# Batch 0's attention in the program's own order on four engines, with the w1 weight slices dealt out one per key chunk

## The chip, the core and the metric

The kernel runs on one core of one Trainium2 chip. The metric is the device time of one execution in microseconds (us), lower is better. Every kernel below was run beside runs of the kernel before on the same chip, and its result was compared with the reference. A run is counted as slow when it is more than 1.5% above the fastest run of the same kernel; such runs are left out of the ratios.

## The reference, cut to what matters

Two blocks follow each other. First comes attention over hashed buckets, 4 batches, 8 heads, 768 positions, head size 64; then a Fourier mixing block with a two-layer network on the 512 columns.

```
q_bits = (q @ proj > 0); k_bits = (k @ proj > 0)      # 6 bits each
mask   = bucket(q) == bucket(k)
scores = where(mask, scale * q @ k.T, -1e9)
attn   = softmax(scores)                               # over the keys
x      = attn @ v            -> (B, S, 512)
...
u  = x + real(fft2(x))                                 # over positions and columns
un = (u - mean(u)) / sqrt(var(u) + 1e-6)
out = u + relu(un @ w_ch1) @ w_ch2                     # w_ch1: 512 x 2048, float64 input
```

## The kernel before

Batch 0's attention goes through four head pairs, each in six key chunks. I call one chunk of one pair a "step"; there are 24. In each step the matrix engine (PE) forms scores for two query halves (`weigh`), ScalarE takes the exponential, and PE applies V to the chunk before it (`values`, in `finish`). For pairs 0 and 1 PE also adds up the softmax's row sums; for pairs 2 and 3 VectorE does, with two additions a step ("accumulations", tile `acc`). Beside this, `prepare` makes the next pair ready in pieces: transposes, bit products on PE, and their evacuation into `qkb` by VectorE.

The second weight of interest, w1, comes as float64, and is narrowed to float32 on the chip in 16 slices of 128 x 512 while batch 0's attention runs:

```
    def narrow(dst, raw, mask):
        lo, hi = (raw.rearrange("p (n w) -> p n w", w=2)[:, :, i] for i in range(2))
        ...
        nc.scalar.activation(mask, hi, AF.Abs)                        # ScalarE, 3 instructions
        nc.scalar.activation(mask, mask, AF.Abs, bias=mid[:, 0:1])
        nc.scalar.activation(mi, mask, AF.Sign, bias=mid[:, 1:2])
        nc.vector.tensor_scalar(di, hi, ...)                          # VectorE, 5 instructions
        nc.vector.scalar_tensor_tensor(mi, di, 1, mi, ...)
        nc.vector.scalar_tensor_tensor(di, hi, -(2**31), mi, ...)
        nc.vector.tensor_scalar(mi, di, -(1 << 23), None, ...)
        nc.vector.scalar_tensor_tensor(rest, lo.bitcast(U32), 2.0**-52, mask, ...)
        nc.gpsimd.tensor_tensor(dst, dst, rest, op=ALU.add)           # GpSimd, 1 instruction
```

After every fourth slice GpSimd adds the four slices up (`ws`), PE multiplies the sum with a constant matrix (`wm`, "the mean product"), and VectorE subtracts the result from the four slices. That removes the mean of each column of w1 once, instead of the mean of `u` in every row later.

```
        for i, (dst, src) in enumerate(slices):
            ...
                narrow(dst, raws[i % len(raws)].bitcast(I32), mask)
            fetch(i + depth, nc.gpsimd)
            yield
            if wsb is w1 and i % NDC == NDC - 1:
                f = i // NDC * WC
                ws = wt([P, WC], F32, "u", f"ws{f}", 2)
                for c in range(1, NDC):
                    nc.gpsimd.tensor_tensor(ws, ..., w1[:, c, f : f + WC], op=ALU.add)
                ps = pt([P, WC], f"wm{f}")
                nc.tensor.matmul(ps, mean, ws, start=True, stop=True)
                for c in range(NDC):
                    w = w1[:, c, f : f + WC]
                    nc.vector.tensor_tensor(w, w, ps, op=ALU.subtract)
                yield
```

The product's result `ps` comes from a PSUM pool of two buffers (`pt`), which it shares with the transposes, the bit products and the sums. The main loop runs the attention as a generator and takes one piece of w1 per step. The order in which each engine gets its instructions is then decided by a scheduler, not by this text:

```
    for b in range(B):
        for _ in attention(b):
            for _ in range(per_step):
                next(other, None)
```

Of the kernel before, what the change touches and what calls it, by code (L numbers as in the profile page):

```python
# [29 lines left out]
NDC = DM // P  # L30
# [435 lines left out]
def _main(  # L466
# [26 lines left out]
    def wt(shape, dtype, tag, name, bufs=2):  # L493
        return work.tile(shape, dtype, tag=tag, name=name, bufs=bufs)

    roomy = [True]
    turn = [0]

    def pt(shape, name):

        turn[0] += 1
        if roomy[0] and turn[0] % 2:
            if turn[0] % 4 == 1:
                return ps_o.tile(shape, F32, tag="o", name=name)
            return ps_sc.tile(shape, F32, tag="sc", name=name)
        return ps_1.tile(shape, F32, tag="ps", name=name)
# [14 lines left out]
    def load(n, others=nc.sync):  # L521
        b, t = divmod(n, NPAIR)
        for nm, src in (("q", q), ("k", k), ("v", v)):
            tag, bufs = ("vn", 2) if nm == "v" else ("qkn", 2)
            tl = wt([P, NT, 2, D], F32, tag, f"{nm}n{n}", bufs)
            for h in range(2):
                (nc.sync if nm == "q" else others).dma_start(
                    tl[:, :, h, :], src[b, 2 * t + h].rearrange("(p c) d -> p c d", c=NT)
                )
            nat[nm, n] = tl  # L530
# [49 lines left out]
    w1 = const.tile([P, NDC, DFF], F32, tag="w1", name="w1")  # L580
# [38 lines left out]
    def weights(wsb, wdr):  # L619

        wide = wdr.dtype == I64
        slices = [
            (wsb[:, c, f : f + WC], wdr[c * P : (c + 1) * P, f : f + WC])
            for f in range(0, wdr.shape[1], WC)
            for c in range(wdr.shape[0] // P)
        ]
        raws, masks = [], []
        if wide:
            zt = wt([P, 3, 2 * WC], F32, "z", f"zraw{wdr.shape[0]}", 1)
            raws += [zt[:, i] for i in range(3)]  # L630
            if wsb is w1:
                ft = wt([P, 12, WC], F32, "F", "fraw", 1)
                raws += [
                    ft[:, i : i + 2].rearrange("p i w -> p (i w)") for i in range(0, 8, 2)
                ]
                masks = [ft[:, i] for i in range(8, 12)]

        def fetch(i, queue):
            if i < len(slices):
                dst, src = slices[i]  # L640
                if wide:
                    raw = raws[i % len(raws)].bitcast(I32)
                    queue.dma_start(raw.bitcast(I64), src)
                else:
                    queue.dma_start(dst, src)

        depth = len(raws) or 4
        for i in range(depth):
            fetch(i, nc.sync if wsb is w1 else nc.gpsimd)
            if wsb is w1 and i == 1:  # L650
                load(1)
        yield
        for i, (dst, src) in enumerate(slices):
            if wide:
                mask = masks[i % 4] if masks else wt([P, WC], F32, "u", f"mask{i}", 2)
                narrow(dst, raws[i % len(raws)].bitcast(I32), mask)
            fetch(i + depth, nc.gpsimd)
            yield
            if wsb is w1 and i % NDC == NDC - 1:

                f = i // NDC * WC
                ws = wt([P, WC], F32, "u", f"ws{f}", 2)
                for c in range(1, NDC):
                    nc.gpsimd.tensor_tensor(
                        ws, ws if c > 1 else w1[:, 0, f : f + WC],
                        w1[:, c, f : f + WC], op=ALU.add,
                    )
                ps = pt([P, WC], f"wm{f}")
                nc.tensor.matmul(ps, mean, ws, start=True, stop=True)
                for c in range(NDC):  # L670
# [3 lines that stand above are left out]
# [128 lines left out]
    def values(n, c, pk, oos):  # L802

        for g in range(2):
            w = HALF + 1 - g
            for h in range(2):
                nc.tensor.matmul(  # L807
                    oos[g][h * D : (h + 1) * D, 0:w], nat["v", n][:, c, h, :],
                    pk[g][:, h, 0:w], start=(c == 0), stop=(c == NT - 1),
                )  # L810
# [44 lines left out]
    def attention(b):  # L855
        xs[b] = wt([P, NPAIR, S], F32, "x", f"x{b}")
        pending, scaling = [], [iter(())]

        def finish():
            n, c, pk, oos, accs, sums = pending.pop(0)  # L860
            for _ in scaling[0]:
                pass
            values(n, c, pk, oos)
            if sums is not None:
                for i in range(4):
                    nc.tensor.matmul(
                        sums[32 * i : 32 * i + 32, :], ones[:, 0:32],
                        pk[i // 2][:, i % 2, 0:HALF],
                        start=(c == 0), stop=(c == NT - 1),
                    )  # L870
            if c == NT - 1:
                scaling[0] = scale(n, oos, accs, sums)
                next(scaling[0], None)

        for t in range(NPAIR):
            n = NPAIR * b + t
            if 1 < n + 1 < NPAIR * B:
                load(n + 1)
            ahead = prepare(n + 1) if n + 1 < NPAIR * B else iter(())
            oos = [ps_o.tile([P, 512], F32, tag="o", name=f"oo{n}_{g}") for g in range(2)]  # L880
            accs = sums = None
            if n in SUMS:
                sums = pt([P, HALF], f"sums{n}")
            else:
                accs = [wt([P, 2, HALF], F32, "t3", f"acc{n}_{g}", 3) for g in range(2)]
            first = None
            for c in range(NT):
                new = [weigh(n, g, c) for g in range(2)]
                if c == 0:
                    first = new  # L890
                elif accs:
                    for g in range(2):
                        nc.vector.tensor_tensor(  # L893
                            accs[g], first[g][:, :, 0:HALF] if c == 1 else accs[g],
                            new[g][:, :, 0:HALF], op=ALU.add,
                        )
                while pending:
                    finish()
                pending.append((n, c, new, oos, accs, sums))
                if c > 0:  # L900
                    next(ahead, None)
                yield
        while pending:
            finish()
        for _ in scaling[0]:
            pass
# [138 lines left out]
    def after(n, one, two):  # L1045

        for _ in range(n):
            next(one)
            yield
        yield from both(two, one)  # L1050



    other, per_step = weights(w1, moe_w_ch1), 1
    next(other)
    nc.sync.dma_start(ch, cn["ch"].ap())
    nc.sync.dma_start(sq, cn["sq"].ap())
    for _ in prepare(0):
        pass
    roomy[0] = False  # L1060
    for b in range(B):
        for _ in attention(b):
            for _ in range(per_step):
                next(other, None)
        if b == B - 1:
            roomy[0] = True

            ms = const.tile([P, 2], F32, tag="ms", name="ms")
            nc.vector.tensor_reduce(ms, norms, axis=AX.X, op=ALU.max)
            ps = pt([1, 2, P], "norms_t")  # L1070
            for io in range(2):
                nc.tensor.transpose(ps[:, io, :], ms[:, io : io + 1], ident)
            mt = const.tile([1, 4], F32, tag="mt", name="mt")
            nc.vector.tensor_reduce(mt[:, 0:2], ps, axis=AX.X, op=ALU.max)
            nc.vector.tensor_tensor(mt[:, 2:3], mt[:, 0:1], mt[:, 1:2], op=ALU.mult)
            fl = const.tile([1, 1], I32, tag="fl", name="fl")
            nc.vector.tensor_scalar(fl, mt[:, 2:3], (SAFE / SCALE) ** 2, None, op0=ALU.is_gt)
            large = nc.values_load(fl[0:1, 0:1], min_val=0, max_val=1)
        for _ in other:
            pass  # L1080
        other, per_step = mix(b), 3
        if b == 0:
            other = after(NPAIR + NT, other, weights(w2, moe_w_ch2))
# [47 lines left out]
```

## Time and profile before

| | kernel before |
|---|---|
| median of the fast runs beside the changed kernel | 1320.5 us |
| profiled span | 1316.3 us |
| PE busy | 1247.1 us, 95% |
| mean granted PE clock | 0.978 |
| batch 0's attention (17.9 to about 177) | 159 us, of which some 115 us is PE work at full clock (an estimate, worked out in the prediction) |

One of its four first runs took 3932.38 us and is left out. Two things in the profile matter beside what the prediction shows. First, the accumulations of pairs 2 and 3 run without disturbance, because by then GpSimd is done with w1 (0.50 and 0.00 us busy in their windows, which the prediction shows). A row of the timeline: start, busy us, engine, line, operation, output and inputs, shape, count, and in brackets the idle time before it and what ended it.

```profile
131.44 1.83 DVE L893 TENSOR_TENSOR acc<-acc,pk 128x768 f32<-128x768 f32 x2 [3.02 <-ACT pk L793]
```

Two accumulations take 1.83 us. Second, PE hardly waits for the mean products. The list of PE's waits in the first 200 us of the kernel before (total us, times, longest us):

```profile
PE bitsq L727 <- DVE qkb L728: 7.7, 1, 7.7
...
PE wm L669 <- issue: 0.2, 1, 0.2
```

The mean products (`wm`) wait 0.2 us. The scheduler puts them where their operand is already there. What PE waits for most (7.7 us in the first row) are evacuations that stand behind narrowing in VectorE's queue.

### The profile page before, as it was taken

The numbers are of one execution on the slowest core, as the hardware profiler recorded it, in microseconds if no ns is written. First come the engines' busy times: TensorE is split into PE (matmuls) and PEld (weight loads), VectorE is DVE, ScalarE is ACT, GpSimd is POOL, SyncE is SP. The second block draws the span as 40 slices with busy tenths as digits, with TensorE's granted clock in tenths as the row PEclk, the third lists the DMA queues.
The fourth block names the chain that finished last, engine by engine and source line by source line (L and its number), as shares of the span: only waits on it lengthen the run. The fifth ranks groups of instructions, "written<-read, shape, count | busy, mean of one in ns | idle before, by whom it ended". The sixth has DMA issues, their size and how long they took to land.

```text
span 1316.3 us, 12158 instructions
## 1 busy us (share of the span) xinstructions
PE 1247.1 (95%) x4776; PEld 623.3 (47%) x4776; DVE 661.1 (50%) x1147; ACT 332.2 (25%) x541; POOL 133.9 (10%) x190
## 2 busy tenths in 40 slices
PE   6679989899999999999999999999999998999997
PEld 3223447344445444654445444755445444854553
DVE  4983777995435438554434636654444635410010
ACT  6544444552122213122121212222112111110000
POOL 2651001430100100000000100000000000001000
PEclk9689999889999999999999999999999999999999
DMA  9311112330110101010010111001010000000000
GB/s 284 108 40 33 41 38 91 119 94 0 29 32 12 32 8 45 0 24 13 20 41 0 24 29 32 12 13 24 8 28 1 1 8 17 0 0 17 8 8 18
DMA packets 82881, 44.65 MB, mean 34 GB/s; under 512 B 76800, under 2 KB 76928, under 8 KB 82688
## 3 DMA queue, kind: packets, MB, share of 16 engines
q1 hardware_dynamic: 74032, 23.61, 7.2%
q0 software_dynamic: 5648, 19.40, 4.4%
q10 hardware_dynamic: 3136, 0.79, 0.3%
q8 instruction: 39, 0.64, 0.2%
q14 instruction: 26, 0.21, 0.1%
HBM read 37.50 MB, written 6.29 MB: 33 GB/s over the span
## 4 chain that ended last, share of the span: by engine, by line
PE 80%; DVE 10%; issue 4%; DMA 3%; POOL 1%; ACT 1%; ACTq 0%; POOLq 0%; SPq 0%; DVEq 0%
PE h L1001 25%; PE o L1029 24%; PE sc L787 10%; PE oo L807 8%; PE cs L950 3%; DVE pk L796 3%; PE B L976 2%; PE A L976 2%; DMA zraw<-in_moe_w_ch_dram 2%; PE sum L845 1%; DVE acc L893 1%; PE trk L701 1%; POOL w L617 1%; PE un L1017 1%; ACT pk L793 1%
## 5 line engine op out<-in xcount | busy, mean ns | idle before, releaser
L1001 PE MATMUL h<-x,w 128*128 128x384 f32 x1024 | 346.9, 496 | 9.6 <-DVE rt L816 3.5
L1029 PE MATMUL o<-w,h 128*128 128x512 f32 x768 | 342.1, 597 | 0.4 <-DVE h L1008 0.4
L1001 PEld LDWEIGHTS h<-x,w 128*128 128x128 f32 x1024 | 193.6, 192 | 158.2 <-issue 15.2
L796 DVE SCALAR_TENSOR_TENSOR pk<-qb,kb,pk 128x384 f32<-128x384 bf16 x264 | 154.8, 625 | 191.2 <-ACT pk L793 191.2
L793 ACT ACTIVATE pk<-sc 128x768 f32<-128x768 f32 x192 | 149.8, 810 | 336.5 <-PE sc L787 252.3
L1029 PEld LDWEIGHTS o<-w,h 128*128 128x128 f32 x768 | 141.5, 190 | 174.2 <-issue 167.9
L787 PE MATMUL sc<-qt,kt 64*128 64x384 f32 x768 | 197.4, 516 | 2.8 <-ACT pk L793 2.8
L807 PE MATMUL oo<-pk,vn 128*64 128x384 f32 (+1 forms) x768 | 153.2, 504 | 1.7 <-DVE x L850 1.2
L1008 DVE TENSOR_SCALAR h<-h 128x384 f32<-128x384 f32 x64 | 35.6, 556 | 168.2 <-PE h L1001 167.9
L787 PEld LDWEIGHTS sc<-qt,kt 64*128 64x128 f32 x768 | 81.0, 189 | 82.4 <-issue 59.3
L893 DVE TENSOR_TENSOR acc<-acc,pk 128x768 f32<-128x768 f32 x112 | 106.3, 954 | 11.1 <-ACT pk L793 9.4
L1010 ACT ACTIVATE h<-h 128x384 f32<-128x384 f32 x64 | 31.3, 489 | 296.4 <-PE h L1001 296.4
L1035 DVE SCALAR_TENSOR_TENSOR u<-o,rs,u 128x512 f32<-128x512 f32 x24 | 18.0, 750 | 150.9 <-PE o L1029 122.5
L807 PEld LDWEIGHTS oo<-pk,vn 128*64 128x64 f32 x768 | 47.7, 136 | 93.8 <-issue 81.4
L1025 POOL TENSOR_SCALAR rs<-mv 128x1 f32<-128x1 f32 x24 | 9.7, 405 | 521.7 <-DVE mv L1023 521.3
L920 POOL DMA_DIRECT2D out_dram<-u x32 | 19.6, 613 | 355.0 <-DVE u L1035 301.3
L950 PE MATMUL cs<-ch,z 128*128 128x256 f32 x192 | 47.9, 400 | 6.8 <-ACT qt L516 2.8
L617 POOL TENSOR_TENSOR w<-w,zraw 128x512 f32<-128x512 f32 x24 | 37.6, 1565 | 89.6 <-DVE zraw L614 89.1
L950 PEld LDWEIGHTS cs<-ch,z 128*128 128x128 f32 x192 | 36.1, 196 | 20.7 <-ACT qt L516 4.6
L1019 ACT COPY u<-un 128x512 f32<-128x512 f32 x24 | 14.1, 587 | 117.7 <-PE un L1017 117.7
L976 PE MATMUL B<-sq,F 128*128 128x193 f32 (+1 forms) x192 | 37.0, 329 | 0.7 <-DVE x L992 0.7
L976 PE MATMUL A<-sq,F 128*128 128x193 f32 (+1 forms) x192 | 36.9, 329 | 0.3 <-DVE x L992 0.3
(119 smaller groups left out, 895.1 us busy)
## 6 DMA issues: line engine op xcount, KB each, us to landing
zraw<-in_moe_w_ch_dram POOLq DMA_DIRECT2D x21, 512.0 KB, 3.7
qn<-in_q_dram SPq DMA_DIRECT2D x32, 192.0 KB, 3.2
vn<-in_v_dram SPq DMA_DIRECT2D x30, 192.0 KB, 3.2
kn<-in_k_dram SPq DMA_DIRECT2D x30, 192.0 KB, 3.2
out_dram<-u POOLq DMA_DIRECT2D x16, 256.0 KB, 2.4
fraw<-in_moe_w_ch_dram SPq DMA_DIRECT2D x4, 512.0 KB, 7.0
fraw<-in_moe_w_ch_dram POOLq DMA_DIRECT2D x4, 512.0 KB, 4.2
out_dram<-u POOLq DMA_DIRECT2D x16, 128.0 KB, 2.5
```

The source lines that it names most:

```text
L617: nc.gpsimd.tensor_tensor(dst, dst, rest, op=ALU.add)
L787: nc.tensor.matmul(ps[:, h, 0:HALF], kt[rows, ks], qt[rows, qs], start=kb is not None, stop=True,)
L793: nc.scalar.activation(pk[:, :, 0:HALF], ps[:, :, 0:HALF], AF.Exp, scale=SCALE)
L796: nc.vector.scalar_tensor_tensor(pk[:, h, 0:HALF], qb[:, h, qs], kb[:, h, c : c + 1], pk[:, h, 0:HALF], op0=ALU.is_equal, op1=ALU.mult,)
L807: nc.tensor.matmul(oos[g][h * D : (h + 1) * D, 0:w], nat["v", n][:, c, h, :], pk[g][:, h, 0:w], start=(c == 0), stop=(c == NT - 1),)
L893: nc.vector.tensor_tensor(accs[g], first[g][:, :, 0:HALF] if c == 1 else accs[g], new[g][:, :, 0:HALF], op=ALU.add,)
L950: nc.tensor.matmul(ps[:, pc:DM:2], z[:, cp, pc, par, t * P : (t + 1) * P], ch[:, cp, pc, :], start=(cp == 0), stop=(cp == 1),)
L976: nc.tensor.matmul(ps[:, cols], f, sq[:, t, k, cols], start=(t == 0), stop=(t == NT // 2 - 1),)
L1001: nc.tensor.matmul(ps, w1[:, c, fc * P : (fc + 1) * P], x[:, c, g * HALF : (g + 1) * HALF], start=(c == 0), stop=(c == NDC - 1),)
L1008: nc.vector.tensor_scalar(hr, ps, 0.0, None, op0=ALU.max)
L1010: nc.scalar.activation(hr, ps, AF.Relu)
L1029: nc.tensor.matmul(ps, hs[fc][:, j * P : (j + 1) * P], w2[:, fc, :], start=(fc == 0), stop=(fc == NFC - 1),)
```

## The change

The intent: keep the scheduler out of batch 0's attention. PE, VectorE, ScalarE and GpSimd get their instructions in the order in which the program states them, one slice of w1 stands in each of four steps and the mean product in the fifth. The evacuations that the attention needs can then no longer end up behind several slices. A second edit moves the `yield`s around the mean's sum, so that the product is asked for one step after the sum.

```
@@ in weights()
             fetch(i + depth, nc.gpsimd)
-            yield
+            if wsb is not w1 or i % NDC < NDC - 1:
+                yield
             if wsb is w1 and i % NDC == NDC - 1:
                 ...            # GpSimd's additions for ws
+                yield
                 ps = pt([P, WC], f"wm{f}")
                 nc.tensor.matmul(ps, mean, ws, start=True, stop=True)
@@ the main loop
-    for _ in prepare(0):
-        pass
-    roomy[0] = False
+    ET = mybir.EngineType
+    with tc.manual_schedule(engines={ET.PE, ET.DVE, ET.Activation, ET.Pool}):
+        for _ in prepare(0):
+            pass
+        roomy[0] = False
+        for _ in attention(0):
+            next(other, None)
+        for _ in other:
+            pass
     for b in range(B):
-        for _ in attention(b):
-            for _ in range(per_step):
-                next(other, None)
+        if b > 0:
+            for _ in attention(b):
+                for _ in range(per_step):
+                    next(other, None)
```

## The prediction

> **What bounds the kernel now.** I read the slices first, for where the matrix engine is not full; then windows for those stretches; then groups of instructions there; last the timeline. The slices (40 of 32.9 us each, in tenths; PE is the matmul row, PEclk the granted clock):
>
> ```profile
> PE   6679989899999999999999999999999998999997
> DVE  4983777995435438554434636654444635410010
> PEclk9689999889999999999999999999999999999999
> ```
>
> The matmul row is at 9 nearly everywhere; only the first four slices show 6 to 7, a low clock in the second and third, and VectorE full in the third. The change touches that place: batch 0's attention, four head pairs of six key chunks, 24 "steps". Each step forms scores for two halves ("weigh"), takes the exponential on ScalarE, and applies V to the chunk before. Beside it the float64 weight w1 is narrowed, 16 slices over ScalarE (3 instructions), VectorE (5) and GpSimd (1). The pairs start at 17.9, 70.7, 122.3 and about 148.8 us, and the last ends near 176.5, by the timeline of the matmuls; the windows on those stretches:
>
> ```profile
> 17.00:71.00 54.00, 38.75 (x178) 14.90 (x179) 44.84 (x61) 34.78 (x59) 31.23 (x26) 0.78 0.51 174
> 70.00:122.00 52.00, 42.77 (x230) 15.65 (x230) 28.93 (x45) 20.98 (x33) 17.60 (x13) 0.90 0.10 23
> 122.00:148.00 26.00, 25.35 (x136) 10.78 (x130) 16.09 (x25) 12.76 (x22) 0.50 (x1) 1.00 0.20 46
> 148.00:176.50 28.50, 27.79 (x158) 12.11 (x158) 23.09 (x39) 13.44 (x22) 0.00 (x0) 1.00 0.19 43
> ```
>
> Columns are busy us (instruction count) of PE, weight loads, VectorE, ScalarE and GpSimd, then clock and transfers. Pairs 2 and 3 take 26 to 28 us with PE full: the limit. Pairs 0 and 1 take 53 and 52 us, with PE busy 39 and 43 and a clock of 0.78 and 0.90.
>
> ```profile
> 35.12 0.90 PE L701 MATMUL trk<-ident,kn 128*128 128x128 f32 x3 [3.09 <-ACT kt L516]
> ...
> 53.09 1.65 PE L727 MATMUL bitsq<-qt,pjw 128*128 128x384 f32 x2 [7.74 <-DVE qkb L728]
> ...
> 116.11 1.51 PE L807 MATMUL oo<-pk,vn 128*64 128x385 f32 x8
> 117.55 0.85 PE L866 MATMUL sums<-pk,ones 128*32 128x384 f32 x8
> 118.34 0.34 PE L782 MATMUL sc<-qkb 64*128 64x384 bf16 x2
> 118.51 0.81 PE L787 MATMUL sc<-qt,kt 64*128 64x384 f32 x4
> ```
>
> The last four rows are a full-speed step: from 116.11 to 120.06, where the next oo group starts, is 3.95 us, of which weigh 1.72, values 1.44, row sums 0.78. Preparing the next pair adds some 4.9 us (transposes 0.9 twice, bit products 1.55 twice). Pairs 0 and 1 thus need 6 x 3.95 + 4.9 + 1.5 (sums for the scaling) = 30 us each, and pairs 2 and 3, whose row sums go to VectorE, 25 to 26. With four w1 products of 1.1 the whole is 115 us against 17.9 to 176.5 = 159: 44 us are lost, all in pairs 0 and 1. That is the ceiling of any gain, 3.3%. The first two rows show the loss: PE waits for an evacuation which stands behind narrowing in an engine's queue.
>
> ```profile
> 10.39 0.43 DVE L602 TENSOR_SCALAR w<-zraw 128x512 int32<-128x512 int32 x1 [2.35 <-DMA zraw<-in_moe_w_ch_dram]
> ...
> 18.39 0.68 DVE L605 SCALAR_TENSOR_TENSOR fraw<-w,fraw 128x512 int32<-128x512 int32 x1
> ...
> 60.61 1.88 DVE L605 SCALAR_TENSOR_TENSOR fraw<-w,fraw 128x512 int32<-128x512 int32 x1
> ```
>
> In the first row VectorE's queue head waits for w1's transfer while batch 0's transposed q waits behind it; and the same instruction takes 0.68 us or 1.88. Groups in the first 180 us, whose idle column tells what each waited for:
>
> ```profile
> L605 DVE SCALAR_TENSOR_TENSOR fraw<-w,fraw 128x512 int32<-128x512 int32 x16 | 17.4, 1095 | 0.3 <-ACT fraw L598 0.3
> L893 DVE TENSOR_TENSOR acc<-acc,pk 128x768 f32<-128x768 f32 x16 | 14.8, 953 | 6.8 <-ACT pk L793 6.8
> L597 ACT ACTIVATE fraw<-fraw,mid 128x512 f32<-128x512 f32 x16 | 11.5, 722 | 0.3
> L617 POOL TENSOR_TENSOR w<-w,zraw 128x512 f32<-128x512 f32 x8 | 13.1, 1640 | 35.6 <-DVE zraw L614 35.6
> L664 POOL TENSOR_TENSOR ws<-ws,w 128x512 f32<-128x512 f32 x8 | 10.9, 1360 | 0.4
> ```
>
> **What the Trainium skill says.** "Perfetto Trace Analysis", Tensor Engine Instruction, says ScalarE, VectorE and GpSimd are strict FIFO, so order alone can delay ready work; the 10.39 row agrees. "SBUF — State Buffer", SBUF: two separate sides, says GpSimd and certain VectorE instructions (two SBUF inputs, or a two-port mode) hold a shared port pair exclusively. The 1.88 us row overlaps GpSimd's addition of 60.63 to 61.92, so the trace agrees: mean 1095 ns against 680 alone. "TensorE: Matmul & The Clock Gate", Why this matters for your kernels, says a PE gap over about 3 us drops the clock to half. Here a 3.09 us gap before 35.12 is followed by a clock of 0.50 from 34 to 42 us, and eight oo products take 2.83 us instead of 1.51.
>
> **The change part by part.** It removes no work. From the changed kernel's built order: PE, VectorE, ScalarE and GpSimd now follow the program for batch 0; slices go at steps 0-3, 5-8, 10-13, 15-18 and the mean products at 4, 9, 14, 19. From pair 3 on the four queues are the same as before but for small swaps, so what happens later is carried over as a shift. I walk the 24 steps in that order by hand with the durations above.
>
> Costs. A slice is 3 x 0.72 = 2.15 us on ScalarE, after that step's two exponentials (1.55) and evacuations; on VectorE 0.43 + 0.72 + 0.73 + 0.46 + 0.69 = 3.0 us in a dependent chain (2.6 after the mask arrives), up to 4.1 with the port conflict (66 us busy for 16 slices now); on GpSimd 1.4, plus 0.9 for issuing the next fetch. The sum for the mean is 3 x 1.31 = 3.9.
>
> Start: without the slice at VectorE's head the bits are ready about 13.5-14 instead of 17.5. **Gain 4 us.**
>
> Pair 0, from 14.0: weigh 0 and 1 to 17.7, values 0 to 19.9; each pair of transposes has one free PSUM buffer, so it costs PE one evacuation, about 0.9 us. Steps 1, 2 and 3 end at 21.8, 28.2 and 35.2; in step 2 the key transposes wait for two exponentials (24.7-26.2) and a norm behind them on ScalarE (to 27.2). Step 3's second bit product waits for VectorE's slice 2, whose mask came at 30.9 and which ends at 33.6. Slice 3 follows on VectorE 35.9-38.9, GpSimd needs 2.3 + 3.9, so the mean's sum is ready at 45.2; PE reaches its product at 41.6 and **waits 3.7**. Pair 1 starts at 50.3, against 70.7. **Gain so far 20 us.**
>
> Pair 1: the scaling of pair 0 sits behind slice 5 on VectorE (57.6-60.6), so PE waits 1.8 + 2.1 + 0.6 us before values 6. Slice 7's chain, ScalarE after the key evacuation (72.95) + 2.15 + 2.65 + 6.2, ends at 84.0; PE has only 6.9 us of work for it and waits 4.8. Pair 2 starts near 95.8 against 122.3. **Gain so far 26 us.**
>
> Pair 2 is where I expect it to be given back. VectorE has now 12 accumulations of 0.95 = 11, five slices of 3.0 = 15, a subtraction of 2.5, bits 2.8 and scaling 3.4: 35 us, 40 with port conflicts, against 25 for PE. In order, pair 1's scaling stands behind slice 10 and two accumulations, so values 12 waits until 109.2 (PE idle from 104.0); slice 11's mask comes after that at 115.2 and the sum at 123.2, PE idle from 116.1; and pair 3's bits are scaled after slice 13 and the accumulations of step 17, near 143. Pair 3 starts at 141-145, against 148.8. **Gain left 4 to 8 us.**
>
> Pair 3: values 17 and sums to 149.4; scaling two halves 5.3 us; slice 15 behind it 3.0; GpSimd 1.4 + 3.9. The last product comes near 163 (now 156.9), PE idle some 7 us before it. The remaining steps are as now, 19 us. The attention ends at 179-184 against 176.5: **a loss of 3 to 7 us**. Six of the waits are over 3 us with the clock gate to follow; each could cost 2 us where PE is then what is waited for, which the walk leaves out. From the walk alone I get 1322 + 5 = 1327. It sums many waits, and I took the longer figure where there were two (3.0 us a slice, where the instructions of interleaved slices now follow each other in 0.6 us); against that stands the clock. I choose 1324.
>
> **Rivals.** (1) The stalls simply vanish: PE runs at 4.5 to 5 us a step throughout, and 20 to 30 us come off (1292 to 1302). For it: pair 0 gains 20 us even in my walk, and VectorE's whole load, 120 us busy in the first 180, would fit. Against: the slices that crowd pairs 0 and 1 now must stand somewhere, and VectorE's 35 to 40 us against 25 in pair 2 are in the group table. (2) The gaps put the clock at half for most of the stretch, and the mean product with 5 us waits costs more: 1340 to 1350. For it: the 3.09 us gap above. Against: when PE waits for VectorE or GpSimd anyway, slow products hide. (3) Something is returned after batch 0: w2's narrowing from 208 us on depends on a buffer freed by mixing, which shifts with everything else, so I expect a rigid shift and no hiding.
>
> **Range and chances.** Walk +5, its pair-2 uncertainty of 5 to 10 us either way, rival 1 at 25 us, rival 2 at +20: 8 in 10 between 1304 and 1341. Faster by over 2% means below 1295.5, which takes 26 of 44 lost us: 0.06. Slower by over 2%, above 1348.4: 0.04.
>
> **What would show it.** In the changed profile: scores from about 14 us; pair 1 starting near 50, pair 2 near 96, pair 3 near 143; PE waits of 3 to 7 us before each mean product, ended by GpSimd's ws sum; waits before values 6 and 12 ended by VectorE's x; VectorE near full from 95 to 155; GpSimd's w1 sums spread to 160. I am wrong if pair 2 runs in 30 us, if the mean products do not wait, or if the shift at 180 us is not the shift at the end.

## The result, and the profile after

The changed kernel took 1336.62 us (median of four fast runs, 1335.14 to 1337.69) beside 1320.5 us for the fast runs of the kernel before. The ratio is 1.0118, with a 95% interval of 1.0099 to 1.0138: slower by 1.2%. All outputs are right. Ratios here and below are the mean time of one kernel's fast runs over that of the kernel before in the same rounds, so they are not quite the ratio of the medians quoted.

The profiled span went from 1316.3 to 1333.3 us, by 17.0. PE busy fell from 1247.1 to 1239.8, so PE's idle time (span less busy) rose from 69.2 to 93.5, by 24.3 us. The slices of the changed kernel's page, 40 of 33.3 us each, in tenths:

```profile
PE   7775688889999999999999999999999998999997
...
DVE  3445875897434636653444626754344535311010
...
PEclk9887889999999999999999999999999999999999
```

The low stretch has not gone; it has moved. The first two slices are better than before and the third is as full (7, 7, 7 against 6, 6, 7, at a clock of 0.9 to 0.8), and slices four and five (100 to 167 us) are worse: 5 and 6, where the kernel before had 9 and 9, at a clock of 0.7 and 0.8. VectorE is at 8 in the fifth. The windows on the head pairs of the changed kernel (pair 0, 1, 2, 3; columns as in the prediction) say it more sharply:

```profile
12.80:50.00 37.20, 29.78 (x174) 11.45 (x173) 17.20 (x30) 22.07 (x36) 11.57 (x11) 0.95 0.65 211
50.00:97.50 47.50, 35.80 (x198) 13.06 (x194) 22.18 (x41) 24.43 (x41) 12.06 (x13) 0.89 0.27 70
97.50:149.20 51.70, 31.66 (x154) 13.12 (x154) 36.72 (x52) 24.63 (x40) 15.96 (x11) 0.80 0.14 33
149.20:193.70 44.50, 33.47 (x168) 14.14 (x170) 32.58 (x50) 17.22 (x29) 8.46 (x5) 0.84 0.12 28
```

Pairs 0 and 1 take 37 and 48 us, where the kernel before took 53 and 52. Pairs 2 and 3 take 52 and 45 us, where it took 26 and 28. At 97.5 us the changed kernel is 25 us ahead; at the end of batch 0's attention it is 15 us behind. The last row sum of pair 3 stands at 192.24 against 177.07.

PE's waits in the first 200 us of the changed kernel:

```profile
PE wm L671 <- POOL ws L665: 25.2, 4, 8.7
PE oo L809 <- DVE x L852: 9.0, 4, 4.8
PE sc L784 <- DVE qkb L735: 7.2, 3, 6.0
```

The four mean products wait 25.2 us, where they waited 0.2 before. That is about the whole rise of PE's idle time (24.3 us); the other gains and losses of PE's idle time cancel. What such a wait looks like in the timeline of PE of the changed kernel:

```profile
118.82 0.38 PE L703 MATMUL trk<-ident,kn 128*128 128x128 f32 x2
127.22 2.08 PE L671 MATMUL wm<-ws,mean 128*128 128x512 f32 x2 [8.02 <-POOL ws L665]
...
129.53 1.49 PE L789 MATMUL sc<-qt,kt 64*128 64x384 f32 x4
```

PE stands 8.02 us, and then the product takes 2.08 us instead of 1.1, and the four score products 1.49 instead of 0.81: half clock. VectorE and GpSimd in the same stretch:

```profile
119.86 0.69 DVE L614 SCALAR_TENSOR_TENSOR fraw<-fraw 128x512 f32<-128x512 uint32 x1
120.47 2.90 DVE L895 TENSOR_TENSOR acc<-acc,pk 128x768 f32<-128x768 f32 x2
129.34 2.48 DVE L674 TENSOR_TENSOR w<-w,wm 128x512 f32<-128x512 f32 x4 [5.96 <-PE wm L671]
```

```profile
120.64 1.92 POOL L617 TENSOR_TENSOR w<-w,fraw 128x512 f32<-128x512 f32 x1 [11.15 <-DVE fraw L614]
122.52 1.97 POOL L665 TENSOR_TENSOR ws<-w 128x512 f32<-128x512 f32 x1
124.57 2.60 POOL L665 TENSOR_TENSOR ws<-ws,w 128x512 f32<-128x512 f32 x2
```

VectorE's part of the fourth slice is done at 120.55. Then GpSimd needs its last addition for the slice, and three more for the sum: from 120.64 to 127.17. The product asks for the sum and starts at 127.22. Two accumulations of VectorE stand beside GpSimd's addition and take 2.90 us instead of 1.83; GpSimd's addition takes 1.92 instead of 1.28 (its row at 101.71, with no accumulation beside it). The figures fit three instructions that run strictly one after the other: the first accumulation of 0.96 us until 121.43; then GpSimd, whose record began 0.17 us after the pair's and ends at 122.56, so 1.13 us of its 1.92; then the second accumulation of 0.96. Together that is 3.0 us, close to the 2.90 measured. The Trainium skill, "SBUF — State Buffer", SBUF: two separate sides, says that of a VectorE instruction with two SBUF inputs and a GpSimd instruction that reads SBUF, the one that starts first holds the shared pair for its whole length and the other one fully blocks; these rows agree.

The groups of instructions in the first 180 us of the changed kernel, which answer to those of the prediction:

```profile
L895 DVE TENSOR_TENSOR acc<-acc,pk 128x768 f32<-128x768 f32 x10 | 12.6, 1281 | 0.9 <-ACT pk L795 0.7
L605 DVE SCALAR_TENSOR_TENSOR fraw<-w,fraw 128x512 int32<-128x512 int32 x16 | 11.9, 743 | 28.7 <-ACT fraw L598 27.8
```

The narrowing instruction that had a mean of 1095 ns before now has 743: the slices no longer run beside GpSimd's additions. The accumulations had 953 and now have 1281. The blocking has moved from the narrowing to the accumulations.

### The profile page after: what moved, and what is told of

It is laid out like the page before. It is cut to its first block, busy times and chain, and to the rows that moved or that the text cites. A ratio compares the mean times of both kernels' runs of the same rounds, so it can differ in the third digit from the quotient of the medians.

```text
span 1333.3 us, 12150 instructions
## 1 busy us (share of the span) xinstructions
PE 1239.8 (93%) x4776; PEld 621.0 (47%) x4776; DVE 655.7 (49%) x1147; ACT 333.9 (25%) x541; POOL 133.3 (10%) x190
## 4 chain that ended last, share of the span: by engine, by line
PE 76%; issue 9%; DVE 8%; POOL 4%; ACT 2%; DMA 1%; POOLq 0%; SPq 0%; ACTq 0%; DVEq 0%
PE h L1003 24%; PE o L1031 24%; PE sc L789 8%; PE oo L809 7%; PE cs L952 3%; DVE pk L798 3%; POOL w L617 2%; PE B L978 2%; PE A L978 2%; POOL ws L665 1%; ACT pk L795 1%; PE sum L847 1%; DVE acc L895 1%; PE un L1019 1%; PE trk L703 1%
## 5 line engine op out<-in xcount | busy, mean ns | idle before, releaser
L1003 PEld LDWEIGHTS h<-x,w 128*128 128x128 f32 x1024 | 192.6, 191 | 159.2 <-issue 13.9
L789 PE MATMUL sc<-qt,kt 64*128 64x384 f32 x768 | 189.6, 522 | 2.8 <-ACT pk L795 2.8
L895 DVE TENSOR_TENSOR acc<-acc,pk 128x768 f32<-128x768 f32 x112 | 109.7, 984 | 10.5 <-ACT pk L795 8.6
L1027 POOL TENSOR_SCALAR rs<-mv 128x1 f32<-128x1 f32 x24 | 6.5, 271 | 521.6 <-DVE mv L1025 521.2
```

The costliest lines, as they stand in the source:

```text
L789: nc.tensor.matmul(ps[:, h, 0:HALF], kt[rows, ks], qt[rows, qs], start=kb is not None, stop=True,)
L895: nc.vector.tensor_tensor(accs[g], first[g][:, :, 0:HALF] if c == 1 else accs[g], new[g][:, :, 0:HALF], op=ALU.add,)
L1003: nc.tensor.matmul(ps, w1[:, c, fc * P : (fc + 1) * P], x[:, c, g * HALF : (g + 1) * HALF], start=(c == 0), stop=(c == NDC - 1),)
```

## The experiments

Eleven further kernels were run. Medians in us; the kernel before was at 1319.2 to 1320.5.

| run | median | range | ratio to before (95%) |
|---|---|---|---|
| changed kernel | 1336.62 | 1335.14-1337.69 | 1.0118 (1.0099-1.0138) |
| yields_back | 1335.42 | 1334.48-1336.59 | 1.0122 (1.0099-1.0144) |
| kept_warm | 1327.85 | 1326.93-1330.28 | 1.0065 (1.0047-1.0083) |
| add_on_vector | 1326.41 | 1323.61-1328.69 | 1.0049 (1.0031-1.0067) |
| running_sum | 1325.22 | 1322.85-1327.67 | 1.0046 (1.003-1.0061) |
| double_pace | 1318.84 | 1317.88-1320.83 | 0.9997 (0.9979-1.0014) |
| scaling_first_early | 1317.91 | 1309.93-1320.23 | 0.9977 (0.9951-1.0002) |
| paced_scheduled (one slow run of 1467.96 left out) | 1315.99 | 1314.64-1317.58 | 0.9970 (0.9952-0.9987) |
| product_later | 1316.27 | 1313.80-1319.51 | 0.9980 (0.9962-0.9998) |
| paced_add_on_vector | 1312.40 | 1311.27-1315.99 | 0.9944 (0.9926-0.9961) |
| scaling_first | 1310.95 | 1306.95-1315.03 | 0.9931 (0.9911-0.9952) |
| product_free_slot | 1308.17 | 1306.28-1308.61 | 0.9906 (0.9892-0.9921) |

My theory after the result: the mean product stands at the head of PE's queue before its operand is there, and what it costs is the wait plus the half clock after it. Rivals: VectorE's whole load with the blocked accumulations is the limit, whatever the place of the products; or the program's order as such is worse than the scheduler's.

### yields_back: the second edit undone

```
-            if wsb is not w1 or i % NDC < NDC - 1:
-                yield
+            yield
...
-                yield
                 ps = pt([P, WC], f"wm{f}")
```

> The second part of the change undone (the sums on GpSimd and the mean's product in one piece again), the program's order kept. As built, all four queues hold the same instructions in the same order as the changed kernel, so the part does nothing by itself: I expect the changed kernel's time, 1336 within 2 us, and the same four waits for the ws sum (25 us in all). If the part had been of use or harmful, the time would differ by 4 us or more.

It measured 1335.42 us, and the four waits are again 25.2 us together. As built, it has the same instructions in the same order on all four engines as the changed kernel, and the two traces show the same: moving GpSimd's additions across a `yield` changes nothing in any single engine's order, because no other GpSimd instruction stands in the step between, and the product and its subtractions keep their places. So "asked for one step later" is only in the text. The product still comes one step after the fourth slice, where it would have come anyway. All of the change's effect is the program's order.

### product_later: the mean product after the second slice of the next group

```
+        late = []
+        def subtract():
+            f, ws = late.pop(0)
+            ps = pt([P, WC], f"wm{f}")
+            nc.tensor.matmul(ps, mean, ws, start=True, stop=True)
+            ...                                    # VectorE's four subtractions
...
+            if late and i % NDC == LATE:           # LATE = 1
+                subtract()
...
+                late.append((f, ws))
-                ps = pt([P, WC], f"wm{f}")
-                nc.tensor.matmul(ps, mean, ws, start=True, stop=True)
```

> As the changed kernel, but each mean product is asked for two steps later still (after the second slice of the next group), all else the same. My theory: the 25.2 us that PE waits for GpSimd's ws sums (3.7, 4.8, 8.0, 8.7) go, and with them the half clock that follows each; in pairs 2 and 3 about half comes back as waits for VectorE, which has 35 to 40 us of work there. So 1336 goes to 1316 to 1323, with pair 0 and 1 shorter by 5 to 7 us each. The rival, that VectorE's load alone sets pairs 2 and 3 and the waits for the sums only show it: less than 10 us come off, 1327 or more.

It measured 1316.27 us, within the expectation, and 19 us below yields_back. The order of the program is not bad in itself; the place of the products was. But the wait was only partly gone. PE's waits in the first 200 us of this run:

```profile
PE wm L653 <- DVE qkb L743: 10.5, 2, 5.5
PE oo L822 <- DVE x L865: 10.1, 4, 4.5
```

The product no longer waits for GpSimd's sum but for `qkb`: two of the four products now stand right behind the bit products, which hold both PSUM buffers until VectorE has evacuated them. One wait had taken the place of another.

### double_pace: the same, with two pieces of w1 per step

```
         for _ in attention(0):
-            next(other, None)
+            for _ in range(2):
+                next(other, None)
```

> As product_later, but two pieces of w1 per key chunk, so that all 16 slices are done in pairs 0 and 1, which have no accumulation on VectorE, and pairs 2 and 3 are free of them. My theory (what is given back comes of slices standing between the accumulations in pairs 2 and 3): pairs 2 and 3 run in 26 us each as in the kernel before, pairs 0 and 1 at 7 to 8 us a step end near 105 us, batch 0's attention ends near 157 to 165 us instead of 193, and the time is 1303 to 1312, under the kernel before. The rival, that program order itself is worse than the scheduler's whatever the pace: 1321 or more.

It measured 1318.84 us, between the two expectations, so neither held. Half of the first came out: pairs 2 and 3 took 25 and 29 us (starts at 123.60 and 148.39, last row sum at 177.01), about as in the kernel before. But pairs 0 and 1 ended near 124 us, not 105. Putting w1 into the first half costs there what it saves in the second, as the scheduler's order had done.

### kept_warm: the changed kernel, with PE kept at work before the four products

```
                 ps = pt([P, WC], f"wm{f}")
+                warmer = sq[:, 0].rearrange("p k n -> p (k n)")[:, 0:WC]
+                for _ in range((3, 4, 7, 8)[f // WC]):
+                    nc.tensor.matmul(ps, mean, warmer, start=True, stop=True)
                 nc.tensor.matmul(ps, mean, ws, start=True, stop=True)
```

The added products are overwritten by the real one; they only fill the wait.

> The changed kernel with 3, 4, 7 and 8 idle products of 1 us each in front of the four mean products, into the same PSUM tile, where PE waits anyhow; it only keeps the matrix clock up. If the half clock after these four waits costs what its slow instructions sum to (about 2 us each), 4 to 8 us come off: 1329 to 1332. If the waits alone count and the slow products hide behind VectorE, the time stays at 1336 within 2 us.

It measured 1327.85 us, 7.6 us below yields_back (which is the changed kernel's instructions in the same order). The third product in the timeline of PE of this run (the first row shows the last 12 of the 14 matmuls that fill the wait; each product is two):

```profile
117.66 5.31 PE L673 MATMUL wm<-sq,mean 128*128 128x512 f32 x12
123.39 1.12 PE L674 MATMUL wm<-ws,mean 128*128 128x512 f32 x2 [0.41 <-POOL ws L665]
...
124.62 0.81 PE L792 MATMUL sc<-qt,kt 64*128 64x384 f32 x4
```

The product is at 1.12 us again and the scores at 0.81. The operand comes no sooner than before, and PE's time until then is now filled; so the half clock alone costs some 7.6 us of the kernel's time. The Trainium skill, "TensorE: Matmul & The Clock Gate", Why this matters for your kernels, which names gaps above about 3 us, agrees with the four gaps of 3.72 to 8.69 us.

### product_free_slot: products at steps where sum and PSUM buffer are both there

```
-        for _ in attention(0):
-            next(other, None)
+        slices = [1, 1, 1, 1, 0, 1, 1, 1, 1, 0, 1, 1, 1, 1, 0, 1, 1, 1, 1, 0, 0, 0, 0, 0]
+        products = (6, 11, 17, 23)
+        for s, _ in enumerate(attention(0)):
+            for _ in range(slices[s]):
+                next(other)
+            if s in products:
+                subtract()
```

The product and its subtractions are again a function `subtract`, and the w1 generator now only does the slices and sums (this part of the edit is left out here). The slices stay in the steps of the changed kernel (0 to 3, 5 to 8, 10 to 13, 15 to 18). Only the products and their subtractions move, from steps 4, 9, 14, 19 to 6, 11, 17, 23.

> The changed kernel with slices at the same steps, products at steps 6, 11, 17 and 23. Against product_later (6, 11, 16, 21) only the last two move, out of the steps in which the bit products hold both PSUM buffers. There PE waited 10.5 us for VectorE's bits in front of the product. If those waits are the buffers' (my theory), 6 to 10 us come off with the clock: 1306 to 1311. If VectorE's load sets pairs 2 and 3 anyway, the time stays at 1314 to 1318.

It measured 1308.17 us, as expected: 28 us below the changed kernel and 12 us below the kernel before (ratio 0.9906). It is the fastest kernel. PE's waits in the first 200 us of this run:

```profile
PE oo L812 <- DVE x L855: 9.3, 4, 3.7
...
PE sc L787 <- DVE qkb L738: 6.1, 2, 5.1
...
PE wm L624 <- DVE qkb L733: 2.3, 1, 2.3
```

The waits for `x` and `qkb` are as in the changed kernel (9.0 and 7.2 there); the one in front of the products has shrunk from 25.2 to 2.3 us. The blocked accumulations are all still there, as VectorE's rows in this run show:

```profile
98.03 2.90 DVE L898 TENSOR_TENSOR acc<-pk,pk 128x768 f32<-128x768 f32 x2
111.11 6.82 DVE L898 TENSOR_TENSOR acc<-acc,pk 128x768 f32<-128x768 f32 x4
121.97 2.91 DVE L898 TENSOR_TENSOR acc<-acc,pk 128x768 f32<-128x768 f32 x2
```

Two take 2.90 or 2.91 us, also at 128.90 and 146.41, and four take 6.82 at 111.11. So the blocked accumulations can't be what makes the changed kernel slower than the kernel before.

### scaling_first and scaling_first_early: free VectorE for the scaling as well

Two attempts to take away the waits for `x` too, by leaving the slice out where a pair's scaling has to run.

```
-        slices = [1, 1, 1, 1, 0, 1, 1, 1, 1, 0, 1, 1, 1, 1, 0, 1, 1, 1, 1, 0, 0, 0, 0, 0]
-        products = (6, 11, 17, 23)
+        slices = [1, 1, 1, 1, 1, 1, 0, 1, 1, 1, 1, 1, 0, 1, 1, 1, 1, 1, 0, 0, 0, 0, 0, 0]   # scaling_first
+        slices = [2, 1, 1, 1, 1, 2, 0, 1, 1, 1, 1, 1, 0, 1, 1, 1, 0, 0, 0, 0, 0, 0, 0, 0]   # scaling_first_early
+        products = (5, 11, 17, 23)
```

> As product_free_slot, but no slice in the three steps (6, 12, 18) in which a pair's scaling starts on VectorE, the slices taken up in steps 4, 9, 14 that had none; first product at step 5. The 10 us that PE waits for VectorE's x (values of the next pair behind a slice and accumulations) should fall to 3 us or less. My theory: another 5 to 8 us off product_free_slot, 1299 to 1305. The rival, that these waits hide behind VectorE's total in pairs 2 and 3: 3 us or less.

> As scaling_first, but two slices in steps 0 and 5, which prepare nothing, so that 13 of the 16 slices stand in pairs 0 and 1 and three in pair 2, none after step 15. My theory (slices between accumulations are what gives the gain back): pairs 2 and 3 run at 26 to 30 us, batch 0's attention ends near 155 us, 1296 to 1302, faster than both kernels. If the two doubled steps stall PE as in double_pace, pairs 0 and 1 grow by 6 us or more and the time is that of scaling_first or worse.

They measured 1310.95 and 1317.91 us, so my theory missed in both: neither beats product_free_slot. The first is not clear of it (the intervals of the ratios overlap, and its runs spread over 8 us); the second is slower. In scaling_first the waits for `x` fell from 9.3 to 3.2 us, but those of the key bit products for `qkb` rose from 4.4 to 9.2, and the sums waited 5.1. In scaling_first_early the alternative of the expectation came true: pair 2 starts some 7 us later than in scaling_first. The scaling's own sums wait 13.9 us for VectorE, 9.0 of it in one place, where VectorE works from 45.3 to 61.0 us almost without a pause, on slices for the most part. With this much work on VectorE, moving a slice moves the wait.

### paced_scheduled: the same pace, with the scheduler's order

The loop of product_free_slot without the line `with tc.manual_schedule(...)`.

> product_free_slot without the manual section: the same program text (slices and products at the same steps), but the scheduler orders the queues again. If the gain of product_free_slot over the kernel before comes of program order with the products out of the way, this is back at the kernel before: 1318 to 1322, pairs 0 and 1 at 50 us each. If the later products alone make the gain, it is 1306 to 1311.

It measured 1315.99 us, between the two expectations and nearer to the first: 4 us below the kernel before, of the 12 that the same text gains with the program's order. Its largest wait is one of 10.2 us before a query bit product and one of 9.0 before a sum, of the same kind as in the kernel before. So with these slots the program's order is worth about two thirds of what product_free_slot gains; the slots alone are worth about a third.

### add_on_vector: the last addition of a w1 slice moved from GpSimd to VectorE

```
-        nc.gpsimd.tensor_tensor(dst, dst, rest, op=ALU.add)
+        adder.tensor_tensor(dst, dst, rest, op=ALU.add)     # VectorE for w1
```

> The changed kernel with the last addition of each w1 slice on VectorE instead of GpSimd, all else the same. In the changed kernel each pair of accumulations in pairs 2 and 3 that follows a slice takes 2.9 us instead of 1.8, and GpSimd's addition beside it 1.9 instead of 1.3. If the two hold each other up, the pairs go back to 1.8, each mean's sum is ready 1 us or more sooner, and with an addition of 0.7 on VectorE 6 to 10 us come off: 1326 to 1331. If the longer times have another cause, VectorE only gains 11 us of work and the time is 1335 or more.

It measured 1326.41 us: the number I had expected if the blocking on the shared port were the cause. But the trace doesn't support that reading. VectorE, then GpSimd, in this run:

```profile
123.55 2.89 DVE L898 TENSOR_TENSOR acc<-acc,pk 128x768 f32<-128x768 f32 x2
...
138.07 1.82 DVE L898 TENSOR_TENSOR acc<-acc,pk 128x768 f32<-128x768 f32 x2
```

```profile
123.77 1.84 POOL L668 TENSOR_TENSOR ws<-ws,w 128x512 f32<-128x512 f32 x1 [11.64 <-DVE w L617]
```

The pair of accumulations still takes 2.89 us, now beside GpSimd's addition for the sum; of the five pairs behind a slice, four are at 2.89 and only the one without a GpSimd instruction beside it (138.07) is at 1.82. What did change is the chain in front of the product. GpSimd had nothing else to do, so it added each slice to the sum as it came, and after the fourth slice one addition of 1.84 us is left instead of four. The wait before this third product is 4.35 us, where it was 8.02.

### running_sum: GpSimd keeps all its additions, and adds to the sum after each slice

This run was made to tell the two readings of add_on_vector apart.

```
+            if wsb is w1:
+                c, f = i % NDC, i // NDC * WC
+                if c == 0:
+                    ws = wt([P, WC], F32, "u", f"ws{f}", 2)
+                else:
+                    nc.gpsimd.tensor_tensor(ws, ..., w1[:, c, f : f + WC], op=ALU.add)
...
-                ws = wt([P, WC], F32, "u", f"ws{f}", 2)
-                for c in range(1, NDC):
-                    nc.gpsimd.tensor_tensor(ws, ..., w1[:, c, f : f + WC], op=ALU.add)
```

> The changed kernel, with GpSimd's additions for the mean of w1 issued one by one, each right after its slice, instead of three in a row after the fourth slice; nothing else moves and no engine does less. The run with each slice's last add on VectorE came 10 us below the changed kernel, but its trace shows the accumulations still at 2.89 us a pair, now beside GpSimd's running sum; so the theory of the port conflict, for which I had made it, is in doubt there. New theory: its gain is the shorter chain in front of each mean product, because with GpSimd otherwise free only one of the three additions is left when the fourth slice is done (the waits before the four products fell from 25.2 to 13.5 us). If so, this run shortens the same chain by two additions of 1.3 us, and has to win most of it too: waits of 15 to 18 us before the four products and 1327 to 1331 us. If the gain was the addition taken off GpSimd, this run stays at 1334 to 1338 us, since GpSimd keeps all its additions and the accumulations beside them stay at 2.9 us.

It measured 1325.22 us, a ratio of 1.0046 against 1.0118 for the changed kernel: 0.7% or 9.5 us less, a little more than I had expected from the chain. PE's waits, then VectorE's row beside the last slice of the third group:

```profile
PE wm L674 <- POOL ws L663: 13.6, 4, 5.5
```

```profile
118.12 2.90 DVE L898 TENSOR_TENSOR acc<-acc,pk 128x768 f32<-128x768 f32 x2
```

The accumulations are as blocked as in the changed kernel. The waits before the products fell from 25.2 to 13.6 us, about as in add_on_vector (13.5). The gain of add_on_vector is therefore that of the shorter chain; taking the addition off GpSimd gave nothing beyond it, net of the 11 us of additions that VectorE took over.

This run also shows a short and a long wait side by side. The first and the third product in the timeline of PE:

```profile
42.82 1.12 PE L674 MATMUL wm<-ws,mean 128*128 128x512 f32 x2 [2.08 <-POOL ws L663]
...
122.20 2.08 PE L674 MATMUL wm<-ws,mean 128*128 128x512 f32 x2 [5.51 <-POOL ws L663]
```

In the changed kernel, product_later, product_free_slot, add_on_vector and running_sum, mean products behind a single wait of 3.60 us or more took 1.97 to 2.08 us, and those behind 2.33 us or less 1.12 to 1.55. Shorter waits close together can cost the clock too: in the changed kernel, waits of 1.15 and 1.99 us before 60.51 were followed by eight value products in 2.77 us instead of 1.51.

### paced_add_on_vector: the same move in product_free_slot

The edit of add_on_vector on top of that of product_free_slot.

> product_free_slot with the same move of the additions to VectorE. If the held-up accumulations are on the path there too, 2 to 6 us come off its 1308: 1302 to 1306, the fastest of all. If VectorE's load is the limit of pairs 2 and 3, nothing or a loss: 1307 to 1311.

It measured 1312.40 us, 4 us slower than product_free_slot and just above the second range. Where the products don't wait for the sum, the shorter chain is worth nothing, and VectorE has 16 additions of some 0.7 us more. Its longest wait for `x` rose from 3.7 to 6.1 us.

## Why the prediction was right, and where its sum was off

The range (1304 to 1341) held. The time was 1336.6, 12.6 us above the 1324 on record and 9.6 above the walk's 1327. The size was not right: the prediction put the loss at 2 us, its walk at 5, and about 16 came. The range held because it was wide enough for the rival with the half clock.

- **Start and pairs 0 and 1: right.** Scores from 12.85 (predicted 14), pair 1 at 50.08 (50.3), pair 2 at 97.52 (95.8). The first two products waited 3.72 and 4.76 us (3.7 and 4.8). The walk along the built order gave these two waits to within 0.1 us.
- **"Pair 2 is where I expect it to be given back": right in kind, too small.** The lag of the changed kernel behind the walk grows along the chain: 1.7 us at the start of pair 2 (97.5 against 95.8), 2.8 when slice 11's mask is there (117.95 against 115.2), 4.0 when the sum is ready (127.2 against 123.2), 6.2 at the start of pair 3 (149.24 against the middle of 141 to 145), 7.7 at the last product (170.70 against 163), and 8 to 13 at the end of the attention (192.24 against 179 to 184). No single link of this chain failed; nearly all were too short.
- **The step that failed: "each could cost 2 us where PE is then what is waited for, which the walk leaves out".** The prediction named the half clock and left it out of the sum. kept_warm shows it to be worth 7.6 us, most of the miss against the walk. The reason it gave under rival 2, that slow products hide when PE waits for others anyway, was wrong here: after a mean product VectorE waits for the product itself (5.96 us at 129.34), and the scores that come next are what the following exponentials and accumulations hang on.
- **"up to 4.1 with the port conflict": put on the wrong instructions.** The prediction priced the conflict on the slices, as in the kernel before. In the program's order the slices are nearly free of it (743 ns against 1095), and the accumulations take it: 2.90 us for two, where it reckoned 0.95 each, five times in pairs 2 and 3, some 5 us of VectorE's time in all (5 x (2.90 - 1.90)). GpSimd's chain for the last sum took 7.3 us (163.32 to 170.64), where the prediction had 1.4 + 3.9 = 5.3. How much of the kernel's time this cost was not isolated. It was not decisive: product_free_slot has it too and is the fastest.
- **"VectorE near full from 95 to 155": wrong.** The load of pair 2 was sized well (36.72 us, where 35 to 40 were reckoned), but it was spread over 51.7 us, so VectorE was busy for 71% of it. Its two longest pauses were 5.57 us for slice 11's mask (before 117.95) and 5.96 us for the mean product. By these pauses, pair 2 hung on the chain of waits rather than on VectorE's load.
- **"PE waits of 3 to 7 us before each mean product, ended by GpSimd's ws sum": right in kind**, 3.72, 4.76, 8.02 and 8.69 us; the last two are longer than said. The walk had 22.6 us in all, and 25.2 came. That these four waits are what makes the change a loss is shown by product_free_slot, which moves only the products and their subtractions and gains 28 us (what the subtractions' new place on VectorE is worth was not tested apart); product_later and running_sum take away part of the wait and gain 19 and 9.5.
- **The choice of 1324 under the walk's 1327** went the wrong way. It set the tighter slices against the clock, and the clock was the larger term.
- **Rivals.** The first (stalls vanish, 1292 to 1302) was not reached by any run, the best being 1308. What stands in its way is probably VectorE's load: in product_free_slot it is busy for 70.5 of the 80 us from 90 to 170, and in the two scaling runs a moved slice moved the wait. No run shows that it is the limit. The second (half clock, 1340 to 1350) had the right mechanism and too large a size. The third was right: from about 193 us on every engine has the same instructions in the same order in both traces, and the shift of 15 us at 192 is close to the 17.0 us of the span.

What stays open: why paced_scheduled keeps only a third of the gain was read from its waits, not tested. And no run took GpSimd's additions away from beside the accumulations without changing something else.

## What to carry to other kernels

When you pin the program's order on an in-order engine, each instruction that depends on a long chain elsewhere becomes a wait for everything behind it, so ask for its result only where both its operand and its output buffer are already there; here that one choice was worth 28 us, more than the whole effect of pinning. A wait of the matrix engine as long as those that went with half clock here (3.6 us and more) should be priced twice, once as idle time and once as slow products after it. And when a run gives the number that your theory expected, look in its trace for the mechanism before you call it shown: add_on_vector hit its number for another reason.

## What the Trainium skill lacked or had wrong

- "SBUF — State Buffer", SBUF: two separate sides, states the exclusive lock, and the traces agree. It gives slowdowns as factors, but doesn't say where the blocked time stands in a profile: it is inside the recorded duration (1.83 to 2.90 us for two accumulations, 1.28 to 1.92 us for GpSimd's addition), and no wait is listed for it.
- "Perfetto Trace Analysis", Per-engine timelines, lists what lies in the recorded window of VectorE and GpSimd instructions, and doesn't mention time blocked on that lock either, though here it makes up a third of both durations.
- "TensorE: Matmul & The Clock Gate", Why this matters for your kernels, advises against gaps above about 3 us and agrees with the product at 2.08 instead of 1.1 us. It doesn't name the remedy for a gap that can't be avoided: 3 to 8 products thrown away before each real one brought 7.6 us.
- No page that I read weighs the order of the program against that of a scheduler. Here the same pace took 1308.17 us in the program's order and 1315.99 in the scheduler's, and the program's order with products asked for too early took 1336.62.
